# The tails of batches 0 and 1 at the head of SyncE's queue, and a new order of the whole program

## The chip, the core and the metric

One core of one Trainium2 chip runs the whole program in one launch. The metric is the device time of one execution in microseconds. The time before is the median of three runs, 277.85 us (277.29 to 281.95).

## The reference, cut to what matters

```
q, k, v: (8 batches, 8 heads, 576 rows, 64), float32
phi(x) = where(x > 0, x, exp(x) - 1) + 1
kv  = sum over rows of phi(k)^T v          # 64 x 64 per head
z   = sum over rows of phi(k)
att = phi(q) kv / (phi(q) z + 1e-6)
x   = att as (4608, 512)
a = x @ w1;  b = x @ w2                    # 512 -> 1024
out = (a * b) @ w3 @ w_out                 # 1024 -> 1024 -> 512
```

## The kernel before

Each batch's 576 rows are cut into a main part of 512 rows (four row groups of 128) and a **tail** of 64 rows. The main part of q, k or v is one load of 1 MB (step `ld`, line 119) into one of five buffers. A tail is 128 KB, fetched as 64 x 8 pieces of 256 bytes; tails of two batches share the 128 partitions of one of four buffers, so there are four pairs (0,1), (2,3), (4,5), (6,7). Step `lr` (line 127) loads one tail, step `lp` (line 135) both tails of a pair as two DMAs.

phi is computed as min(max(x, 0) + 1, exp(x)): `x` and `xr` are the exponential on ScalarE (main part and tail), `t` and `tr` the max-and-add on VectorE, `m` and `mr` the minimum on VectorE. `v` and `vr` copy v beside a column of ones, so that `kv` (TensorE) sums kv and z in one product: four matmuls over the main part and one over the tail, for each pair of heads. `kc` and `kh` copy the sums out of PSUM. So `kv` of a batch needs the tail of that batch too.

q is transposed by TensorE for batches 0 to 2 (`qt`, `qc`), by a DMA transpose on SyncE's queue for 3 to 7 (`qd`); `na` multiplies by kv, `nd` (VectorE) divides, and the result is transposed again, by TensorE (`xp`, copied by `xc`) for batches 0 to 2, by DMA (`xd`) for the others. Tails of q go the same way in pairs (`qdr`, `nar`, `ndr`, `xdr`).

w3 @ w_out is made once at the start (`l3`, `lo`, `w3t`, `w3c`, `wa`, `wf`, `wc`), so that the feed-forward part has two products. Chunks 0 to 7 are the batches' main parts, chunk 8 all tails. `f:c,i` (line 393) is one of eight column blocks of chunk c: four matmuls for a and four for b; `ac` (ScalarE) copies a out of PSUM, `ab` (VectorE) multiplies by b. `o:c,m` (line 418) is eight matmuls into 128 output rows; `oc` copies and `st` stores them. The first block of chunk 0 is cut into pieces (`fk`), each started when its part of the transposed input is there. The PSUM pool that f, o, qt, xp and w3t share has four buffers.

All steps stand in one string, ORDER (line 451); each engine and each DMA queue executes its instructions in the order of that string, and only data, buffers and semaphores make it wait. GATES (line 522) adds waits by hand: in `A<B` the load A is issued only when step B is done. SyncE's queue (`,s`) takes most loads, all stores and all DMA transposes; GpSimd's queue (`,g`) takes the weights and the loads of batches 0 and 1, with at most eight DMAs under way.

Of the kernel before, what the change touches and what calls it, by code (L numbers as in the profile page):

```python
# [18 lines left out]
def kernel(  # L19
# [437 lines left out]
    w3c:5,a l3:7 t:k,0,0,4 wf:4 wc:2,v wc:1,a wc:3,a lw:0,0,256 t:k,0,4,4 x:k,0,0,4 wf:5 wc:4,v
    x:k,0,4,4 lw:1,0,256 m:k,0,0,0 m:k,0,0,1 x:q,0,0,4 m:k,0,4,2 t:q,0,0,4 wc:5,a lw:0,1,256 m:q,0,0,1
    x:q,0,4,4 m:q,0,0,0 m:k,0,4,3 qt:0,0,2 t:q,0,4,4 wc:0,a lw:1,1,256 m:q,0,4,2 qc:0,0,2,v lw:0,1,512
    v:0,4,2,a v:0,0,4,v kv:0,2 lw:1,1,512 v:0,6,2,a m:q,0,4,3 kh:0,2,1,a kv:0,1 kh:0,2,0,v kv:0,0 kv:0,3  # L460
    ld:k,1,0,8,g kc:0,0,1,0,a kc:0,0,1,1,v w3t:6 kh:0,3,1,a kh:0,3,0,v na:0,1 na:0,0 w3c:6,a qt:0,2,2
# [100 lines left out]
```

## Time and profile before

| | |
|---|---|
| runs, median (lowest to highest) | 277.85 us (277.29 to 281.95) |
| profiled execution, its own time | 276.11 us |
| its span in the trace | 274.3 us |
| mean granted TensorE clock | 0.960 of 2.4 GHz |
| TensorE / VectorE / ScalarE busy | 243.8 / 164.1 / 125.4 us |
| TensorE in its last stretch, 161 to 270 us | 108.5 us busy of 109 |

The trace is of one execution. Its span reaches from the first to the last instruction; the execution's own time holds 1.8 us more than that. The median of the three runs is 1.7 us above the profiled execution's time. A busy TensorE is a modelled figure, since matmuls are pipelined; a row's idle time (in brackets) names what ended it. A granted clock of 1.00 is 2.4 GHz, one of 0.50 is 1.2 GHz; a value between them is a mean over a stretch that holds both.

### The profile page before, as it was taken

How to read it: one execution, taken by the hardware profiler on the slowest of the kernel's cores; microseconds unless marked ns; L12 is line 12 of the kernel's file. 1: busy time of each engine (PE TensorE's matmuls, PEld its weight loads, DVE VectorE, ACT ScalarE, POOL GpSimd, SP SyncE). 2: the span in 40 equal slices, each digit the busy share in tenths (PEclk: the TensorE clock that was granted, in tenths of full speed). 3: DMA queues.
4: the chain of work that ended last, by engine and by line, in shares of the span. 5: the costliest groups of instructions: out<-in, count | busy, mean ns of one | idle time of the engine just before them, and what ended most of it. 6: DMA issues, size and time to landing. Idle time of an engine off the chain costs nothing.

```text
span 274.3 us, 3971 instructions
## 1 busy us (share of the span) xinstructions
PE 243.8 (89%) x1456; PEld 126.2 (46%) x1474; DVE 164.1 (60%) x366; ACT 125.4 (46%) x190; POOL 21.1 (8%) x35
## 2 busy tenths in 40 slices
PE   6795890998999998779999599999999999999994
PEld 6552740445544553344444244564544444444551
DVE  7308551388998695679899829855975343440110
ACT  3438331478787574364327257823223323333231
POOL 8555500010000000000000000000000000000000
PEclk9999597799999999799999989999999999999998
DMA  6999999896999948999994994891281121003245
GB/s 114 201 291 319 197 260 305 113 352 198 295 273 350 349 145 199 248 220 189 347 265 140 206 307 103 166 182 38 43 163 44 41 59 38 0 2 115 76 133 135
DMA packets 69074, 49.53 MB, mean 181 GB/s; under 512 B 39232, under 2 KB 62016, under 8 KB 69056
## 3 DMA queue, kind: packets, MB, share of 16 engines
q1 hardware_dynamic: 61792, 37.63, 54.2%
q0 software_dynamic: 7120, 11.54, 18.7%
q8 instruction: 11, 0.18, 0.3%
q10 hardware_dynamic: 144, 0.13, 0.1%
q14 instruction: 7, 0.06, 0.1%
HBM read 38.80 MB, written 9.44 MB: 176 GB/s over the span
## 4 chain that ended last, share of the span: by engine, by line
PE 57%; DMA 18%; DVE 15%; issue 4%; ACT 4%; SPq 1%; POOL 1%; DVEq 0%; POOLq 0%; ACTq 0%
PE a_ps L393 19%; PE b_ps L393 17%; PE o_ps L418 14%; DMA k32r<-in_k_dram 4%; DMA k<-in_k_dram 4%; DMA xt<-xn 3%; DVE ab L412 3%; DMA q<-in_q_dram 3%; DVE t L172 3%; DVE xn L299 2%; DMA w3b<-in_moe_w_dram 2%; PE kvp L238 2%; ACT e L166 2%; DVE q L180 2%; DMA q32r<-in_q_dram 2%
## 5 line engine op out<-in xcount | busy, mean ns | idle before, releaser
L393 PEld LDWEIGHTS <-w_sb 128*128 128x128 bf16 x576 | 56.4, 100 | 77.6 <-issue 17.8
L412 DVE TENSOR_TENSOR ab<-a_sb,b_ps 128x512 bf16<-128x512 f32 x72 | 49.1, 684 | 50.5 <-PE b_ps L393 45.8
L393 PE MATMUL a_ps<-xt,w_sb 128*128 128x512 bf16 x256 | 69.0, 391 | 10.7 <-ACT xt L338 7.3
L407 ACT COPY a_sb<-a_ps 128x512 f32<-128x512 f32 x72 | 41.9, 584 | 63.3 <-PE a_ps L393 62.1
L393 PE MATMUL b_ps<-xt,w_sb 128*128 128x512 bf16 x256 | 68.0, 387 | 0.0
L418 PE MATMUL o_ps<-wf_sb,ab 128*128 128x512 bf16 x265 | 63.6, 379 | 2.9 <-DVE ab L412 2.3
L418 PEld LDWEIGHTS <-ab 128*128 128x128 bf16 x280 | 26.3, 98 | 31.8 <-DVE ab L412 3.9
L424 ACT COPY o_sb<-o_ps 128x512 f32<-128x512 f32 x25 | 14.5, 585 | 24.5 <-PE o_ps L418 22.6
L299 DVE TENSOR_TENSOR xn<-nd,r 128x512 bf16<-128x512 f32 x32 | 22.1, 691 | 1.1
L166 ACT ACTIVATE e<-q 128x1024 bf16<-128x1024 f32 x16 | 16.8, 1057 | 9.0 <-DMA q<-in_q_dram 4.9
L166 ACT ACTIVATE e<-k 128x1024 bf16<-128x1024 f32 x16 | 16.5, 1055 | 3.8 <-DVE q L180 2.0
L172 DVE TENSOR_SCALAR t<-k 128x1024 bf16<-128x1024 f32 x16 | 10.8, 685 | 8.1 <-DMA k<-in_k_dram 8.1
L180 DVE TENSOR_TENSOR q<-t,e 128x512 bf16<-128x512 bf16 x32 | 12.7, 419 | 3.9 <-DMA qt<-q 3.1
L291 PE MATMUL nd<-kvb,qt 128*128 128x130 bf16 x128 | 12.2, 226 | 2.3 <-DMA qt<-q 2.2
L238 PE MATMUL kvp<-vt,k 128*128 128x130 bf16 x128 | 11.9, 231 | 2.5 <-ACT vt L217 1.0
L291 PEld LDWEIGHTS <-qt 128*128 128x128 bf16 x128 | 9.3, 100 | 8.3 <-DMA qt<-q 2.6
L180 DVE TENSOR_TENSOR k<-t,e 128x512 bf16<-128x512 bf16 x32 | 12.5, 420 | 0.9 <-ACT e L166 0.7
L238 PEld LDWEIGHTS <-k 128*128 128x128 bf16 x128 | 9.3, 102 | 5.5 <-issue 1.7
L172 DVE TENSOR_SCALAR t<-q 128x1024 bf16<-128x1024 f32 x16 | 10.8, 687 | 1.5 <-DMA q<-in_q_dram 1.4
L424 DVE COPY o_sb<-o_ps 128x512 f32<-128x512 f32 x10 | 6.9, 688 | 7.8 <-PE o_ps L418 7.8
L217 ACT CAST vt<-v 128x1024 bf16<-128x1024 f32 (+1 forms) x11 | 10.1, 932 | 1.9 <-PE kvp L238 1.7
L298 DVE RECIPROCAL r<-r 128x8 f32<-128x8 f32 (+1 forms) x40 | 8.1, 202 | 1.4
(68 smaller groups left out, 187.5 us busy)
## 6 DMA issues: line engine op xcount, KB each, us to landing
out_dram<-o_sb SPq DMA_DIRECT2D x31, 256.0 KB, 3.0
k<-in_k_dram SPq DMA_DIRECT2D x6, 1024.0 KB, 7.0
q<-in_q_dram SPq DMA_DIRECT2D x6, 1024.0 KB, 8.0
v<-in_v_dram SPq DMA_DIRECT2D x6, 1024.0 KB, 8.0
w3b<-in_moe_w_dram POOLq DMA_DIRECT2D x8, 256.0 KB, 8.3
v<-in_v_dram POOLq DMA_DIRECT2D x3, 512.0 KB, 11.0
out_dram<-o_sb SPq DMA_DIRECT2D x9, 128.0 KB, 2.4
k32r<-in_k_dram SPq DMA_DIRECT2D x8, 128.0 KB, 4.9
```

The costliest lines, as they stand in the source:

```text
L166: return nc.scalar.activation(out=e[:, 0:nh * W], in_=raw[n, b][:, h0 * W:(h0 + nh) * W], func=AF.Exp)
L172: nc.vector.tensor_scalar(out=d[:, 0:nh * W], in0=raw[n, b][:, h0 * W:(h0 + nh) * W], scalar1=0.0, scalar2=1.0, op0=ALU.max, op1=ALU.add)
L180: nc.vector.tensor_tensor(out=d[:, hp].rearrange("p j u d -> p u j d"), in0=ts[n, b, h0][:, s].rearrange("p (u j d) -> p u j d", u=2, j=NJ ...
L217: copy_of[eng](out=vts[b % len(vts)][:, :, h0:h0 + nh, 0:D], in_=raw["v", b].rearrange("p (h j d) -> p j h d", h=H, j=NJ)[:, :, h0:h0 + nh])
L238: nc.tensor.matmul(dst, kj[:, hp, j].rearrange("p u d -> p (u d)"), vt[:, j, 2 * hp:2 * hp + 2, :].rearrange("p h e -> p (h e)"), start=(j ...
L291: nc.tensor.matmul(o[:, j // 2, (j % 2) * 256:(j % 2) * 256 + PW], sb["qt", b][:, hp, j * P:(j + 1) * P], kvb[b][:, hp].rearrange("p u e - ...
L299: nc.vector.tensor_tensor(out=dst, in0=o[:, :, :, 0:D], in1=r.unsqueeze(3).to_broadcast(list(r.shape) + [D]), op=ALU.mult)
L393: nc.tensor.matmul(o, w[:, kc, f * P:(f + 1) * P], xt_of(c)[:, :, kc, :], start=(kc == 0), stop=(kc == KC - 1))
L407: return copy_of[eng](out=d, in_=ps["a", c, f])
L412: nc.vector.tensor_mul(out=d[:, f, :], in0=sb["a", c, f], in1=ps["b", c, f])
L418: nc.tensor.matmul(d, sb["ab", c][:, f, m * P:(m + 1) * P], wf_sb[:, f, :], start=(f == 0), stop=(f == FC - 1))
L424: return copy_of[eng](out=d, in_=ps["o", c, m])
```

## The change

The multiset of steps stays the same: the same loads, matmuls, copies and stores, with the same tiles and sizes. Three things differ.

First, the four tail loads of batches 0 and 1 stand at the head of SyncE's queue. Before, the two of batch 1 were held by gates until the last w3 transpose was copied out (`w3c:7`).

Second, all seven old gates are gone (six on tails, one on the second half of v of batch 1); one is new: the main part of q of batch 2 waits until that of q of batch 1 has landed.

Third, the order of all steps is another, and 52 copies change between ScalarE (`a`) and VectorE (`v`), about as many one way as the other.

```
...
-    const:4 lr:k,0,s l3:0 zr:0,1 lr:v,0,s const:0 const:10 const:1 warm:26,0 const:6 l3:1 const:8 l3:2
...
+    const:8 lr:k,0,s l3:0 const:6 lr:v,0,s l3:1 zr:0,0 lr:k,1,s const:0 const:9 l3:2 warm:26,0 lr:v,1,s
...
-    GATES = "lr:k,1,s<w3c:7,a lp:k,1,s<w3c:7,a lr:v,1,s<w3c:7,a lp:v,1,s<ac:0,2,a ld:v,1,4,4,g<ac:0,5,a lp:q,0,s<ac:2,6,a lp:q,1,s<ac:4,3,a"
+    GATES = "ld:q,2,0,8,s<ld:q,1,0,8,g"
```

How the order moves instructions is shown at three places. In a row, `k32r` and `v32r` are tails of k and v, `k_660` and the like main parts, `er` the exponential of a tail, `xt` the transposed input of a chunk.

SyncE's queue at the start of the program, before the change:

```order
L127 DMA k32r<-in_k_dram 64x8x64
L127 DMA v32r<-in_v_dram 64x8x64
L127 DMA k32r<-in_k_dram 64x8x64
L135 DMA k32r<-in_k_dram 64x8x64 x2
L127 DMA v32r<-in_v_dram 64x8x64
L135 DMA v32r<-in_v_dram 64x8x64 x2
L119 DMA k_660<-in_k_dram 128x8x256
```

and with it:

```order
L127 DMA k32r<-in_k_dram 64x8x64
L127 DMA v32r<-in_v_dram 64x8x64
L127 DMA k32r<-in_k_dram 64x8x64
L127 DMA v32r<-in_v_dram 64x8x64
L119 DMA q_672<-in_q_dram 128x8x256
L135 DMA k32r<-in_k_dram 64x8x64 x2
L135 DMA v32r<-in_v_dram 64x8x64 x2
L119 DMA v_785<-in_v_dram 128x8x256
```

The third and fourth tails now stand right behind the first two, with nothing to wait for; the pair (2,3) stands behind the first main part (q of batch 2).

ScalarE around the copies of chunk 0's transposed input, before (kvb is kv of batch 0, a_sb the first a of the feed-forward part):

```order
L365 COPY w3t<-w3p 128x1024 x2
L386 CAST wf_sb<-wf_ps 128x512
L338 COPY xt<-xtp 128x4x128 x2
L194 ACTIVATE er<-k32r 64x512
L338 COPY xt<-xtp 128x4x128
L407 COPY a_sb<-a_ps 128x512 x3
```

With the change, at the start of its program (w3A is the first transposed blocks of w3, vrz the tails of v):

```order
L194 ACTIVATE er<-k32r 64x512
L365 COPY w3A<-w3p 128x1024 x3
L225 CAST vrz<-v32r 64x8x64
L194 ACTIVATE er<-k32r 64x512
L225 CAST vrz<-v32r 64x8x64
```

and around those copies:

```order
L259 CAST kvb_113<-kvp 64x65 x3
L365 COPY w3t<-w3p 128x1024
L338 COPY xt<-xtp 128x4x128
L386 CAST wf_sb<-wf_ps 128x512 x2
L407 COPY a_sb<-a_ps 128x512 x4
```

The exponential of batch 1's tail has gone from between the copies of chunk 0 to the start of the program; three of the four xt copies are VectorE's now.

SyncE's queue in the middle of the program, at the load of v of batch 6 (v_1361 before, v_1746 with the change). Before:

```order
L135 DMA q32r<-in_q_dram 64x8x64 x2
L135 DMA k32r<-in_k_dram 64x8x64 x2
L135 DMA v32r<-in_v_dram 64x8x64 x2
L119 DMA v_1361<-in_v_dram 128x8x256
L135 DMA v32r<-in_v_dram 64x8x64 x2
L279 DMA_TRANSPOSE qt<-q 128x16x128
L343 DMA_TRANSPOSE xt<-xn 128x16x128
```

With the change:

```order
L343 DMA_TRANSPOSE xt<-xn 128x16x128
L279 DMA_TRANSPOSE qt<-q 128x16x128
L436 DMA out_dram<-o_sb 128x512 x2
L135 DMA q32r<-in_q_dram 64x8x64 x4
L119 DMA v_1746<-in_v_dram 128x8x256
L135 DMA q32r<-in_q_dram 64x8x64 x2
L119 DMA k_1794<-in_k_dram 128x8x256
L119 DMA v_1826<-in_v_dram 128x8x256
```

The load of v of batch 6 now stands behind two DMA transposes, two stores and four tails of q.

## Rows read from the trace of the kernel before

**Rows 1.** The page, parts 1 and 2: busy time, and TensorE's in 40 slices.

```profile
PE 243.8 (89%) x1456; PEld 126.2 (46%) x1474; DVE 164.1 (60%) x366; ACT 125.4 (46%) x190; POOL 21.1 (8%) x35
...
PE   6795890998999998779999599999999999999994
```

**Rows 2.** Chain of waits, 30 to 52 us: start, us, what.

```profile
35.26 11.50 DMA k32r<-in_k_dram
...
46.79 0.63 ACT er L194
...
47.44 0.59 ACT xt L338
```

**Rows 3.** TensorE's instructions in time, 40 to 54 us: start, us, group, idle before.

```profile
40.60 0.38 PE L393 MATMUL b_ps<-xt,w_sb 128*128 128x512 bf16 x1
48.08 0.58 PE L393 MATMUL a_ps<-xt,w_sb 128*128 128x512 bf16 x1 [7.10 <-ACT xt L338]
...
51.67 1.03 PE L393 MATMUL a_ps<-xt,w_sb 128*128 128x512 bf16 x4
52.53 1.03 PE L393 MATMUL b_ps<-xt,w_sb 128*128 128x512 bf16 x4
```

**Rows 4.** SyncE's own waits: who for whom, us, times, longest.

```profile
SPq L127 <- ACT w3t L365: 33.1, 1, 33.1
```

**Rows 5.** Table of stretches: us, busy by engine, granted clock, DMA share, GB/s.

```profile
0.00:4.00 4.00, 2.00 (x19) 2.00 (x20) 2.85 (x7) 1.28 (x1) 2.90 (x10) 1.00 0.43 86
4.00:8.00 4.00, 2.72 (x25) 2.28 (x23) 3.51 (x10) 2.08 (x3) 3.44 (x6) 1.00 1.07 167
20.00:24.00 4.00, 3.40 (x16) 1.37 (x14) 3.50 (x7) 3.38 (x6) 2.05 (x3) 1.00 1.03 349
48.08:51.67 3.59, 3.59 (x10) 1.29 (x10) 0.75 (x2) 1.17 (x2) 0.00 (x0) 0.59 1.01 106
111.65:115.92 4.27, 4.27 (x15) 1.60 (x13) 3.43 (x11) 1.75 (x3) 0.00 (x0) 0.60 0.96 219
157.44:160.53 3.09, 3.09 (x8) 1.08 (x8) 0.00 (x0) 1.14 (x2) 0.00 (x0) 0.55 1.08 354
```

**Rows 6.** TensorE's instructions in time, later stretches.

```profile
64.87 0.39 PE L238 MATMUL kvp<-vt,k 128*128 128x130 bf16 x4
...
65.15 0.39 PE L238 MATMUL kvp<-vt,k 128*128 128x130 bf16 x4
...
76.72 1.04 PE L393 MATMUL a_ps<-xt,w_sb 128*128 128x512 bf16 x4
...
111.18 0.63 PE L291 MATMUL nd<-kvb,qt 128*128 128x130 bf16 x8 [2.16 <-DMA qt<-q]
...
123.68 4.71 PE L418 MATMUL o_ps<-wf_sb,ab 128*128 128x512 bf16 x21 [1.61 <-DVE ab L412]
...
157.44 1.86 PE L393 MATMUL a_ps<-xt,w_sb 128*128 128x512 bf16 x4 [3.25 <-DMA xt<-xn]
```

**Rows 7.** ScalarE's instructions in time, 108 to 125 us.

```profile
115.70 0.63 ACT L194 ACTIVATE er<-q32r 128x512 bf16<-128x512 f32 x1 [2.15 <-DMA q32r<-in_q_dram]
```

**Rows 8.** GpSimd's queue in time, the main part of q of batch 1.

```profile
30.32 0.89 POOL L119 DMA_DIRECT2D q<-in_q_dram  x1 [0.36 <-issue]
```

**Rows 9.** The q tiles: DMA transposes (ns shortest/median/longest), and landing times of q loads.

```profile
L279 SPq DMA_TRANSPOSE qt<-q x5: 1993/5462/6934, 103.6 to 174.1; - x5
...
DMA to landing us min/median/max: 5.8/8.0/16.9
```

**Rows 10.** SyncE's queue in time: start, us of issuing, transfer, count.

```profile
52.23 0.48 SPq L119 DMA_DIRECT2D k<-in_k_dram  x1
...
161.93 7.04 SPq L135 DMA_DIRECT2D q32r<-in_q_dram  x6
```

**Rows 11.** The k tiles: landing times of k loads.

```profile
DMA to landing us min/median/max: 5.7/8.0/14.8
```

**Rows 12.** The v tiles: landing times of v loads.

```profile
DMA to landing us min/median/max: 5.6/10.0/18.8
```

More of the change, by code (lines that the diff above doesn't have):

```diff
@@ L457 @@
[L457 to L461, printed above, removed]
@@ new lines @@
+    const:3 l3:3 xr:k,0,0 lo:0,2 const:1 const:4 const:11 lo:2,2 w3t:0 zr:0,1 const:5 warm:8,1 lo:4,2
+    w3c:0,a tr:k,0,0 mr:k,0,0 lo:6,2 const:7 const:2 l3:4 const:10 l3:5 w3t:1 warm:8,2 w3c:1,a
+    ld:k,0,0,4,g w3t:2 warm:8,3 w3c:2,a ld:k,0,4,4,g w3t:3 vr:0,a warm:8,4 w3c:3,v ld:q,0,0,4,g wa:0,1
+    wa:1,1 ld:q,0,4,4,g wa:2,1 xr:k,0,1 tr:k,0,1 mr:k,0,1 wa:3,1 ld:v,0,0,4,g wa:4,1 wa:5,1 ld:v,0,4,2,g
+    vr:1,a wa:6,1 ld:v,0,6,2,g w3t:4 wa:7,1 w3c:4,a l3:6 w3t:5 wc:0,v wc:2,a wf:4 w3c:5,a wc:1,v l3:7
@@ new lines @@
+    xp:0,0 w3t:7 nd:0,2 xc:0,0,a wf:6 ld:v,1,0,4,g w3c:7,v xp:0,1 ld:v,1,4,4,g wf:7 wc:6,a xc:0,1,v
+    na:0,3 xp:0,2 wc:7,a fk:0,0,0,2 nd:0,3 xc:0,2,v xp:0,3 fk:0,0,2,1 xc:0,3,v fk:0,0,3,1 ac:0,0,a f:0,1
+    ab:0,0 ac:0,1,a f:0,3 ab:0,1 ac:0,3,a f:0,5 ab:0,3 ac:0,5,a f:0,7 ab:0,5 x:k,1,0,4 t:k,1,4,4
+    t:k,1,0,4 ac:0,7,a f:0,2 m:k,1,0,1 x:k,1,4,4 m:k,1,0,0 ab:0,7 ac:0,2,a m:k,1,4,2 f:0,6 x:q,1,0,4
+    ld:q,2,0,8,s m:k,1,4,3 ab:0,2 lp:k,1,s x:q,1,4,4 t:q,1,0,4 f:0,4 m:q,1,0,1 ac:0,6,a v:1,0,4,v ab:0,6
@@ new lines @@
+    xp:1,3 st:0,0,s v:2,4,4,a xp:1,2 vr:3,v o:0,1 xc:1,3,v xc:1,2,a m:q,2,0,1 mr:k,1,2 oc:0,3,a
+    ld:v,3,0,8,s v:2,0,4,v vr:2,a f:1,3 m:q,2,0,0 oc:0,1,v ac:1,3,a st:0,3,s t:k,2,4,4 x:k,2,4,4
+    st:0,1,s f:1,0 t:k,2,0,4 x:k,2,0,4 ab:1,3 ld:q,3,0,8,s m:k,2,4,2 ac:1,0,a qt:2,0,2 m:k,2,0,1 f:1,1
+    m:k,2,4,3 qc:2,0,2,a m:k,2,0,0 t:k,3,4,4 x:k,3,0,4 t:k,3,0,4 kv:2,1 ab:1,0 kv:2,3 ac:1,1,a
+    ld:q,4,0,8,s kv:2,0 x:k,3,4,4 kv:2,2 ab:1,1 f:1,6 m:k,3,0,0 kc:2,0,2,1,a m:k,3,4,2 v:3,0,4,a
+    kc:2,0,2,0,v m:k,3,0,1 na:2,3 m:k,3,4,3 na:2,1 ac:1,6,a f:1,4 nd:2,3 v:3,4,4,a ld:v,4,0,8,s nd:2,1
@@ new lines @@
+    ac:1,4,a ab:1,6 xp:2,3 na:2,0 kv:3,1 xc:2,3,a ab:1,4 f:1,7 nd:2,0 x:q,3,0,4 lp:k,2,s t:q,3,0,4
+    ac:1,7,a xp:2,0 m:q,3,0,0 f:1,2 x:q,3,4,4 ab:1,7 xc:2,0,v ac:1,2,a m:q,3,0,1 t:q,3,4,4 x:q,4,4,4
+    xp:2,1 lp:v,2,s na:2,2 ab:1,2 f:1,5 xc:2,1,a m:q,3,4,3 x:q,4,0,4 nd:2,2 ac:1,5,a t:q,4,0,4 kv:3,0
+    xp:2,2 kv:3,2 m:q,3,4,2 xc:2,2,a kv:3,3 ab:1,5 qd:3 o:1,3 kc:3,0,2,1,a t:q,4,4,4 kc:3,0,2,0,a
+    v:4,4,4,a v:4,0,4,v f:2,4 oc:1,3,a st:1,3,s ac:2,4,a f:2,0 xr:k,2,2 tr:k,2,2 ab:2,4 mr:k,2,2
@@ new lines @@
+    na:4,3 oc:1,2,a na:4,0 f:2,7 nd:4,3 st:1,2,s nd:4,0 ac:2,7,a ld:q,5,0,8,s na:4,1 na:4,2 ab:2,7 o:2,2
+    nd:4,1 x:k,5,4,4 t:k,5,4,4 ld:v,5,0,8,s f:3,5 t:k,5,0,4 x:k,5,0,4 oc:2,2,v xr:q,0,2 tr:q,0,2
+    st:2,2,s m:k,5,4,2 ac:3,5,a f:3,4 mr:q,0,2 m:k,5,0,1 ab:3,5 ld:q,6,0,8,s ac:3,4,a m:k,5,4,3 o:2,0
+    m:k,5,0,0 ab:3,4 xr:k,3,2 tr:k,3,2 x:q,5,4,4 t:q,5,4,4 f:3,1 oc:2,0,v x:q,5,0,4 qdr:0 mr:k,3,2
+    m:q,5,4,2 ac:3,1,a nd:4,2 f:3,2 st:2,0,s ab:3,1 v:5,4,4,a xd:4 v:5,0,4,v ac:3,2,a f:3,6 m:q,5,4,3
@@ new lines @@
+    nar:1 ab:4,4 f:4,0 ab:4,6 ac:4,0,a ndr:1 na:5,3 m:q,6,0,0 f:4,7 xdr:0 nd:5,3 ac:4,7,a ab:4,0 qd:6
+    x:k,6,0,4 t:k,6,0,4 f:4,2 tr:q,1,2 xr:q,1,2 m:k,6,0,1 ac:4,2,a ab:4,7 x:k,6,4,4 kv:6,1 t:k,6,4,4
+    f:4,5 ab:4,2 xd:5 m:k,6,4,3 ac:4,5,a m:k,6,4,2 m:k,6,0,0 kv:6,3 kv:6,2 ab:4,5 o:4,2 v:7,4,4,a
+    mr:q,1,2 tr:q,2,2 xr:q,2,2 o:4,0 mr:q,2,2 oc:4,2,a qdr:1 tr:q,3,2 xr:q,3,2 qdr:2 kv:6,0 oc:4,0,v
+    o:4,1 kc:6,0,2,1,a v:7,0,4,a st:4,2,s st:4,0,s kc:6,0,2,0,a o:4,3 oc:4,1,v st:4,1,s na:6,1 oc:4,3,a
@@ new lines @@
+    m:q,7,4,3 qd:7 f:5,0 oc:3,0,a ac:5,0,a st:3,0,s nar:6 nar:7 ab:5,0 f:5,4 ndr:7 ac:5,4,a ndr:6 f:5,7
+    ab:5,4 xdr:3 ac:5,7,a na:6,2 nar:4 ab:5,7 f:5,1 ndr:4 ac:5,1,a nd:6,2 xdr:2 f:5,6 ab:5,1 xd:6
+    ac:5,6,a na:7,1 na:7,3 ab:5,6 o:5,1 nd:7,3 nd:7,1 o:5,3 oc:5,1,a st:5,1,s na:7,0 oc:5,3,v o:5,0
+    nd:7,0 st:5,3,s na:7,2 oc:5,0,v o:5,2 nd:7,2 st:5,0,s xd:7 f:6,6 oc:5,2,v ac:6,6,a st:5,2,s f:6,7
+    ab:6,6 ac:6,7,a f:8,0 ab:6,7 ac:8,0,a f:6,3 ab:8,0 ac:6,3,a f:8,1 ab:6,3 ac:8,1,a f:7,7 ab:8,1
@@ new lines @@
+    ac:7,7,a f:7,6 ab:7,7 ac:7,6,a f:7,4 ab:7,6 ac:7,4,a f:6,2 ab:7,4 ac:6,2,a f:8,3 ab:6,2 ac:8,3,a
+    f:7,5 ab:8,3 ac:7,5,a f:6,4 ab:7,5 ac:6,4,a f:8,2 ab:6,4 ac:8,2,a f:8,6 ab:8,2 ac:8,6,a f:7,2 ab:8,6
+    ac:7,2,a f:7,0 ab:7,2 ac:7,0,a f:7,3 ab:7,0 ac:7,3,a f:6,5 ab:7,3 ac:6,5,a f:7,1 ab:6,5 ac:7,1,a
+    f:8,5 ab:7,1 ac:8,5,a ol:7,3 ab:8,5 o:7,2 o:7,0 oc:7,2,a st:7,2,s o:7,1 oc:7,0,a st:7,0,s f:8,7
+    oc:7,1,v st:7,1,s ac:8,7,a f:6,1 ab:8,7 ac:6,1,a f:8,4 ab:6,1 ac:8,4,a f:6,0 ab:8,4 ac:6,0,a o:8,1
@@ L521 @@
+    ab:6,0 o:6,3 oc:8,1,a st:8,1,s o:8,3 oc:6,3,a st:6,3,s o:8,0 oc:8,3,v st:8,3,s o:8,2 oc:8,0,a
+    st:8,0,s o:6,1 oc:8,2,a st:8,2,s o:6,0 oc:6,1,a st:6,1,s o:6,2 oc:6,0,a st:6,0,s oc:6,2,v st:6,2,s
     """
[L522 removed]
+    GATES = "ld:q,2,0,8,s<ld:q,1,0,8,g"
     ctx.enter_context(tc.manual_schedule())
```

88 lines of the change are left out of this document (25 added, 63 removed).

## The prediction

> **What bounds the kernel now.** The page comes first. TensorE is busy 243.8 of 274.3 us, and its slices stand at 9 nearly everywhere after the first third; the slice that reads 0 is the seventh, near 41 to 48 us [rows 1]. From 161 us on it hardly pauses. So the time is TensorE's own work plus the places at which it stands still, and these are looked for next.
>
> The chain of waits shows the largest place: a 128 KB tail of k takes 11.50 us from its issue at 35.26 to its landing, then 0.63 us of exponential on ScalarE, then a 0.59 us copy of the transposed input [rows 2]. TensorE's own rows show it from the other side: a matmul at 40.60, the next at 48.08, after 7.10 us idle that the copy ended [rows 3]. The copy needs nothing of that tail. It stands behind the tail's exponential on ScalarE, which works in order, and the exponential waits for the DMA. The tail is late because SyncE held it 33.1 us behind the last w3 copy [rows 4].
>
> The table of stretches shows what the pause costs besides. From 48.08 to 51.67 the granted clock is 0.59, a mean of the two levels of 1.2 and 2.4 GHz, and TensorE had stood still for the 7 us before [rows 5]. At full clock the same work takes 0.59 x 3.59 = 2.1 us, so 1.5 us are lost. The whole pause is worth 7.1 + 1.5 = 8.6 us.
>
> Three later pauses have the same form: 2.16 us behind a DMA transpose of q, 1.61 us behind VectorE's product, 3.25 us behind a DMA transpose of x [rows 6]; two are followed by stretches at 0.60 and 0.55, which lose 0.40 x 4.27 = 1.7 and 0.45 x 3.09 = 1.4 us [rows 5]. The second starts on ScalarE, which stands still 2.15 us for a tail of q [rows 7]. Together they cost 10.1 us.
>
> **What the change does, part by part.** No matmul, copy or byte is added or removed, so the sum is about pauses.
>
> *The tails of batch 1.* They no longer wait. ScalarE's exponential of that tail moves to the start of the program, and three of four copies of chunk 0's transposed input go to VectorE. The first feed-forward block then follows its last transpose, copied on VectorE: two more matmuls and a copy after 40.60 come to about 41.3 us. Seven whole blocks stand ready behind it; before, they ran on without a pause once TensorE had restarted.
>
> *The price at the head.* Two more tails, 256 KB in pieces of 256 bytes, go ahead of weights and k. Below: nothing, since the 16 DMA engines are busy only 0.43 in the first 4 us. Above: the rate of the crowded stretch from 4 to 8 us, 167 GB/s, gives 262 KB / 167 = 1.6 us; the best later stretch, 349 GB/s, gives 0.75 [rows 5]. I take 1.2, nearer to the crowded row, because small pieces belong there. The start of chunk 0 is fed by these loads, so all of it is on the path: restart at 41.3 + 1.2 = 42.5. The Trainium skill, "DMA: Bandwidth & Descriptors" (Anatomy of one DMA), prices the moving part at bytes over 436 GB/s, by which this term would be 0.6 us and the sum 0.6 us better; its Specifications say that pieces under 512 B do not reach line rate, which speaks for the upper end and against putting tails first. The trace of before, at 167 GB/s with 256-byte pieces in flight, leans to the second, though casting weight loads run in the same stretch.
>
> *The gain at the first pause.* Before, the restart counts as 48.08 + 1.5 = 49.6 at full clock; with the change, 42.5. That is 7.1 us, between 5.5 (restart at 44.0) and 8.6 (restart at 41.0).
>
> *What is late next.* The main parts of batch 1: GpSimd issues the q at 30.32, and at the longest landing of any q load, 16.9 us, it is there at 47.2 [rows 8, 9]; with 1.2 us for the two tails, 48.4. k is issued ahead of it. Their use stands behind four and six blocks, 7 and 10 us after the restart, so after 49.5. The new gate on q of batch 2 opens with that landing, before 52.23, where SyncE's first main load was issued before [rows 10]. So the loads of batch 2 come no later than now, and I cost them at nothing; if that gate opened 10 us late, ScalarE's exponential of q of batch 2 would stand in the way of stores and copies.
>
> *The three later pauses.* Before the first use of batch 3's q, the order now puts one output step and four blocks, 5 x 1.73 us (a block is two pieces, the first of which takes 52.53 - 51.67 = 0.86 [rows 3]) against 2.0 to 6.9 us of issuing a transpose and a short landing [rows 9]: gone. The tail of q is asked for about ten steps ahead of its exponential: gone. Between the division that feeds chunk 4's transpose and the first block of chunk 4 stand about six steps, 10 us, with another transpose beside it: mostly gone. So 10.1 us can fall away.
>
> *What stands in their place.* SyncE's queue is one line for loads, stores and transposes, and the new order puts main loads behind both. I price the tightest: v of batch 6. VectorE casts it ahead of a product of chunk 4. The last minimum on q of batch 5, which releases the transpose ahead of that load, precedes this cast by seven steps and about seven small groups of four matmuls (0.28 each [rows 6]): 7 x 1.73 + 2.0 = 14.1 us of cover. In that time SyncE must issue the transpose (2.0 to 6.9 us [rows 9]), two stores (1 us), four tails of q (four sixths of 7.04 = 4.7 at most, four times 0.48 = 1.9 at least) and the load, which lands in 5.6 us at the shortest and 10.0 in the median [rows 10, 12]: between 10.5 and 22.6. So it is 3.6 us early to 8.5 us late; I take 2.5 us late, the middle, and 1.4 us of low clock behind it. Two more loads stand like it, k of batch 5 behind a transpose and a store, and k of batch 7 behind four stores; each has about as much cover as its 5.7 to 8.0 us of landing [rows 11], and I take 1.5 us for each, between 0 and 4. That makes 6.9 us, between 2 and 18. The later pauses thus go from 10.1 to 6.9.
>
> *VectorE and ScalarE.* Between chunk 0 and chunk 1 both stay close to full; the copies that change sides are about as many each way and 0.1 us apart. Nothing is taken for them.
>
> **The sum.** 274.3 - 7.1 - 3.2 = 264.0 us of span. The profiled execution took 276.1 with 1.8 us around its span, so 265.8; the median of the runs stands 1.7 us above that. Forecast: **267.5 us**, 3.7% less. Its own range: restart at 41.0 and 2 us of new pauses give 257.7 of span, 261 in the median; restart at 44.0 and 10 us give 268.7, or 272.
>
> **The rivals.** All times are medians (span plus 3.5).
>
> *The first pause goes, the later ones only change place.* Pauses of 10 to 12 us: 274.3 - 7.1 + 1 = 268.2, so 271.7. For it: the order before also left 10.1 us that way. Chance 0.17.
>
> *The gain is given back in the middle.* Pauses of 12 to 19 us, if v of batch 6 and k of batch 5 and 7 come 4 to 5 us late each with 1.4 us of low clock behind: some 17 us, 274.3 - 7.1 + 7 = 274.2, so 277.7. Against it: the longest issues of before fell where loads of 1 MB were under way, and the price above takes their middle already. [...] Chance 0.14.
>
> *Slower.* The mechanism is one: SyncE's line is stopped by a step that needs TensorE's progress, and TensorE needs the load behind it. The place is v of batch 6. It decides from the point where issue and landing together pass the 14.1 us of cover; each us after that is a us of the whole, because the cast sits ahead of VectorE's products. Slower by over 2% (5.6 us) needs 7.1 + 10.1 + 5.6 = 22.8 us of pauses: the 8.5 us at the far end of that sum, and the same at two later loads of the line, 25.5 us or 286.2. Chance 0.05.
>
> *The change doesn't do what it says.* The tails land early but the blocks cannot start, because weights of columns 512 on arrive late (their loads were issued last) or the head is slower than 1.6 us. Then the first pause stays, say 7 of 8.6 us: 274.3 - 1.6 - 3.2 = 269.5, so 273.0. Against it: before, seven blocks ran on the same weights without a wait as soon as TensorE restarted. Chance 0.09.
>
> **How the numbers follow.** The forecast has 0.55. A measurement here can tell about 2%, so the bounds are 272.3 and 283.4. Faster: 0.54 of the forecast, 0.12 of the first rival and 0.03 of the last, 0.69. Within: the rest of these (0.01, 0.05, 0.06) and the second rival, 0.26. Slower: 0.05. The range 261 to 276.5 leaves out the slower case, some 0.05 below and 0.09 of the second rival.
>
> **What would show it.** Right: tails of batch 1 landed before 10 us; no 7 us pause near 41; the first full block at 42 to 44 at a granted clock of 1.00; chunk 1's first block near 67 to 69 instead of 76.7 [rows 6]; the tail of the trace, all matmuls, unchanged in length. Wrong: a new pause between 41 and 55 that ends on a weight or on k or q of batch 1; pauses over 12 us in sum between 100 and 165 that end on a main load through ScalarE or VectorE.

## The result and the profile after

| | before | after |
|---|---|---|
| runs, median (lowest to highest) | 277.57 us (276.03 to 281.95, 4 runs) | 260.49 us (259.28 to 261.56, 4 runs) |
| ratio, 95% interval | | 0.940 [0.934, 0.947] |
| profiled execution / its span | 276.11 / 274.3 us | 260.57 / 258.8 us |
| mean granted clock | 0.960 | 0.986 |

6% faster, where 3.7% was forecast; the median lies 0.5 us under the low end of the range. The page answers [rows 1]: TensorE's busy time fell by 4.0 us and its share rose from 89 to 93%, and the slice that read 0 is gone.

```profile
PE 239.8 (93%) x1474; PEld 125.4 (48%) x1474; DVE 162.2 (63%) x362; ACT 126.3 (49%) x194; POOL 21.7 (8%) x35
...
PE   5589499999999999999999799999999999999993
```

SyncE's queue in time, against [rows 4]: the first line is the tail of batch 1's k, the second that of its v, and nothing holds them. They landed 11.8 and 14.3 us after these issues, at 14.0 and 17.2 us.

```profile
2.22 0.64 SPq L127 DMA_DIRECT2D k32r<-in_k_dram  x1
2.90 0.66 SPq L127 DMA_DIRECT2D v32r<-in_v_dram  x1
```

TensorE's rows at the place of [rows 3] (start, us, group): the last piece of the first block starts at 42.80 and whole blocks run from 43.23. There is no idle time in brackets.

```profile
42.21 0.38 PE L393 MATMUL a_ps<-xt,w_sb 128*128 128x512 bf16 x1
42.43 0.38 PE L393 MATMUL b_ps<-xt,w_sb 128*128 128x512 bf16 x1
42.80 0.38 PE L393 MATMUL a_ps<-xt,w_sb 128*128 128x512 bf16 x1
43.01 0.38 PE L393 MATMUL b_ps<-xt,w_sb 128*128 128x512 bf16 x1
43.23 1.02 PE L393 MATMUL a_ps<-xt,w_sb 128*128 128x512 bf16 x4
```

All later places at which TensorE stood still for 0.3 us or more, and chunk 1's first block (76.72 in [rows 6], now 67.42):

```profile
56.68 0.39 PE L238 MATMUL kvp<-vt,k 128*128 128x130 bf16 x4 [0.35 <-ACT kvb L248]
...
67.42 1.03 PE L393 MATMUL a_ps<-xt,w_sb 128*128 128x512 bf16 x4
...
86.23 0.40 PE L333 MATMUL xtp<-ident,xn 128*128 128x128 bf16 x4 [0.39 <-DVE xn L299]
...
141.95 1.02 PE L393 MATMUL a_ps<-xt,w_sb 128*128 128x512 bf16 x4 [0.41 <-DVE ab L412]
...
147.20 0.40 PE L238 MATMUL kvp<-vt,k 128*128 128x130 bf16 x4 [1.64 <-DVE k L180]
...
167.24 0.40 PE L238 MATMUL kvp<-vt,k 128*128 128x130 bf16 x4 [0.37 <-DVE k L180]
168.71 0.40 PE L291 MATMUL nd<-kvb,qt 128*128 128x130 bf16 x4 [0.45 <-DVE xnr L299]
```

They come to 3.6 us in all. Where [rows 6] has 2.16, 1.61 and 3.25 us, nothing of 0.3 us or more stands now. The table of stretches shows the granted clock behind the first restart, over 100 to 165 us and behind the longest pause left: 1.00 in each, against 0.59, 0.60 and 0.55 in [rows 5].

```profile
43.23:55.31 12.08, 12.08 (x57) 5.49 (x56) 8.49 (x16) 8.45 (x13) 0.00 (x0) 1.00 0.94 283
100.00:165.00 65.00, 62.76 (x377) 31.50 (x375) 49.32 (x115) 32.83 (x50) 0.00 (x0) 1.00 1.02 253
147.20:150.00 2.80, 2.80 (x24) 1.60 (x25) 2.80 (x7) 1.35 (x2) 0.00 (x0) 1.00 1.05 220
```

The loads did come late, as forecast. ScalarE's rows (first k of batch 5, then v and k of batch 6, then k of batch 7) and VectorE's cast of v of batch 6, with the idle time ahead of each:

```profile
111.97 2.01 ACT L166 ACTIVATE e<-k 128x1024 bf16<-128x1024 f32 x2 [1.47 <-DMA k<-in_k_dram]
...
140.60 1.05 ACT L217 CAST vt<-v 128x1024 bf16<-128x1024 f32 x1 [1.50 <-DMA v<-in_v_dram]
...
144.96 1.06 ACT L166 ACTIVATE e<-k 128x1024 bf16<-128x1024 f32 x1 [1.36 <-DMA k<-in_k_dram]
...
165.02 2.00 ACT L166 ACTIVATE e<-k 128x1024 bf16<-128x1024 f32 x2 [1.45 <-DMA k<-in_k_dram]
```

```profile
140.60 0.69 DVE L217 CAST vt<-v 128x1024 bf16<-128x1024 f32 x1 [1.33 <-DMA v<-in_v_dram]
```

Set beside TensorE's rows, these four stops cost it 0, 0.41, at most 1.64 and 0.37 us. That is the point at which forecast and trace part, and the experiments go there.

### The profile page after: what moved, and what is told of

Its sections match the earlier page's. It is cut to its first block, busy times and chain, and to the rows that moved or that the text cites. A ratio compares the mean times of both kernels' runs of the same rounds, so it can differ in the third digit from the quotient of the medians.

```text
span 258.8 us, 3980 instructions
## 1 busy us (share of the span) xinstructions
PE 239.8 (93%) x1474; PEld 125.4 (48%) x1474; DVE 162.2 (63%) x362; ACT 126.3 (49%) x194; POOL 21.7 (8%) x35
## 4 chain that ended last, share of the span: by engine, by line
PE 61%; DVE 15%; DMA 11%; ACT 5%; issue 4%; SPq 2%; POOL 1%; DVEq 0%; ACTq 0%; POOLq 0%
PE o_ps L418 18%; PE a_ps L393 17%; PE b_ps L393 17%; DMA wo<-in_moe_w_out_dram 5%; DVE ab L412 3%; DVE xn L299 3%; DMA q<-in_q_dram 3%; DMA v<-in_v_dram 3%; PE kvp L238 3%; DVE t L172 2%; DVE q L180 2%; ACT e L166 2%; PE nd L291 1%; PE wf_ps L381 1%; DVE r L298 1%
## 5 line engine op out<-in xcount | busy, mean ns | idle before, releaser
L393 PEld LDWEIGHTS <-w_sb 128*128 128x128 bf16 x576 | 55.5, 98 | 63.7 <-issue 1.0
L393 PE MATMUL a_ps<-xt,w_sb 128*128 128x512 bf16 x256 | 66.0, 379 | 0.5 <-DVE ab L412 0.4
L393 PE MATMUL b_ps<-xt,w_sb 128*128 128x512 bf16 x256 | 66.0, 379 | 0.0
L424 ACT COPY o_sb<-o_ps 128x512 f32<-128x512 f32 x23 | 13.4, 584 | 23.7 <-PE o_ps L418 23.7
L424 DVE COPY o_sb<-o_ps 128x512 f32<-128x512 f32 x12 | 8.3, 689 | 21.3 <-PE o_ps L418 16.8
L217 ACT CAST vt<-v 128x1024 bf16<-128x1024 f32 (+1 forms) x12 | 11.1, 946 | 2.9 <-DMA v<-in_v_dram 2.0
```

The source lines that it names most:

```text
L217: copy_of[eng](out=vts[b % len(vts)][:, :, h0:h0 + nh, 0:D], in_=raw["v", b].rearrange("p (h j d) -> p j h d", h=H, j=NJ)[:, :, h0:h0 + nh])
L393: nc.tensor.matmul(o, w[:, kc, f * P:(f + 1) * P], xt_of(c)[:, :, kc, :], start=(kc == 0), stop=(kc == KC - 1))
L424: return copy_of[eng](out=d, in_=ps["o", c, m])
```

## The experiments

Times are medians beside runs of the kernel before on the same chip (276.1 us for experiments 1, 2, 4 and the first timing of 6; 277.4 for 3, 5, 7 and the first timing of 9; 277.3 for 8 and the second timings). A first **whole block** is the first one that is not cut into pieces. In the diffs ORDER is cut to what moves, and the places that a step has left are not always shown.

**1. The tails alone, in the order before.**

```
-    ... zr:0,1 lr:v,0,s const:0 ...
+    ... zr:0,1 lr:v,0,s lr:k,1,s lr:v,1,s const:0 ...
-    GATES = "lr:k,1,s<w3c:7,a lp:k,1,s<w3c:7,a lr:v,1,s<w3c:7,a lp:v,1,s<ac:0,2,a ...
+    GATES = "lp:k,1,s<w3c:7,a lp:v,1,s<ac:0,2,a ...
```

> The order of before, with only the four tails of batches 0 and 1 at the head of SyncE's queue. Theory (ScalarE's line): the first pause of 7.1 us goes, TensorE restarts at 42.5 to 43.5 at full clock, and the later pauses stay: 277.6 - 6.5 = 271 us, between 269 and 273. Rival (the new order as a whole is what pays): under 3 us, 275 or more.

Measured: 270.8 us (270.3 to 272.4), ratio 0.981 [0.975, 0.988]. TensorE's rows: the 7.10 us are gone. The three later pauses stand (2.16, 1.40 and 3.04 us); the longest one between is the second line, 1.10 us where 0.65 stood before.

```profile
43.27 0.38 PE L393 MATMUL a_ps<-xt,w_sb 128*128 128x512 bf16 x1 [0.24 <-ACT xt L338]
...
57.74 1.25 PE L418 MATMUL o_ps<-wf_sb,ab 128*128 128x512 bf16 x5 [1.10 <-DVE ab L412]
```

So early tails are enough to remove the first pause, and that is about a third of the gain.

**2. The exponential moved, the tail still late.** In the order before, `xr`, `tr` and `mr` of batch 1's k go behind the fourth block of chunk 0.

```
-    xr:k,0,1 tr:k,0,1 xp:0,3 fk:0,0,2,1 mr:k,0,1 xc:0,3,a ...
+    xp:0,3 fk:0,0,2,1 xc:0,3,a ...
-    ... f:0,7 ab:0,1 xr:k,1,2 tr:k,1,2 ...
+    ... f:0,7 ab:0,1 xr:k,0,1 tr:k,0,1 mr:k,0,1 xr:k,1,2 tr:k,1,2 ...
```

> The order of before with its late tail; only the exponential, max-and-add and minimum of batch 1's tail of k are moved behind the fourth block of chunk 0, so they no longer stand ahead of the copies. Theory (the line, not the tail's lateness, is what costs): restart at about 41.3, 8 us saved, 269.5 us, between 268 and 272. Rival (the tail has to come early): kv of batch 1 or the exponential's place behind it waits instead, under 3 us saved, 275 or more.

Measured: 274.8 us (271.4 to 275.6), ratio 0.989 [0.978, 1.001]: missed. Whole blocks did start at 42.09, but four blocks later TensorE stood still again. TensorE first, then ScalarE:

```profile
42.09 1.02 PE L393 MATMUL a_ps<-xt,w_sb 128*128 128x512 bf16 x4
...
54.64 1.86 PE L393 MATMUL a_ps<-xt,w_sb 128*128 128x512 bf16 x4 [5.48 <-ACT a_sb L407]
```

```profile
46.80 0.63 ACT L194 ACTIVATE er<-k32r 64x512 bf16<-64x512 f32 x1 [1.33 <-DMA k32r<-in_k_dram]
53.48 0.63 ACT L194 ACTIVATE er<-k32r 128x512 bf16<-128x512 f32 x1 [6.06 <-DMA k32r<-in_k_dram]
```

The moved exponential (64 partitions) waits 1.33 us; the next in ScalarE's line, of the tails of batches 2 and 3 (128 partitions), waits 6.06 us. A stop in an in-order line that is removed uncovers the next late load in that line.

**3. Both late exponentials moved.** The second one goes behind chunk 1's `kh` copies.

```
-    ... ab:0,1 xr:k,1,2 tr:k,1,2 ac:0,7,a ...
+    ... ab:0,1 xr:k,0,1 tr:k,0,1 mr:k,0,1 ac:0,7,a ...
-    ... kh:1,3,0,v kh:1,2,0,v
+    ... kh:1,3,0,v kh:1,2,0,v xr:k,1,2 tr:k,1,2
```

> The order before, with the exponential (and its small followers) of BOTH late tails of k moved on ScalarE: the first (batch 1) to stand behind the fourth block of chunk 0, the second (batch 2) behind chunk 1's kv copies. The tails themselves are still asked for where they were. Theory (a pause is a stop of ScalarE's in-order line at an exponential whose tail has not landed; the earlier run moved one such exponential and the next late tail took its place): restart near 41.5 to 42, no pause of several us near 54, and both stops gone, about 8 us off 276.1: 268 us (266 to 270), pauses near 105 to 155 as before. Rival (the stop is not ScalarE's line but something else that is late by then, weights or the main k and q of batch 1): a pause of 4 us or more still stands between 40 and 60 and less than 3 us is saved: 273 or more.

Measured: 270.6 us (269.9 to 274.4), ratio 0.977 [0.968, 0.986], some 6.5 us less and 0.6 above the expected range. Whole blocks start at 41.14, and the 5.48 us are gone. The profiled execution is the longest of the four, and in it the third late tail, of batch 1's v, stood next (landed 18.0 us after its issue). TensorE, then VectorE:

```profile
58.32 1.89 PE L418 MATMUL o_ps<-wf_sb,ab 128*128 128x512 bf16 x4 [4.29 <-DVE ab L412]
```

```profile
54.74 0.43 DVE L225 CAST vrz<-v32r 64x512 bf16<-64x512 f32 x1 [3.55 <-DMA v32r<-in_v_dram]
```

The rival, weights or main loads, is out: the rows on TensorE's path name a tail each time. Its sign, a pause of over 4 us, did appear, but behind a tail.

**4. One later pause alone.** In the order before, SyncE issues the DMA transpose of chunk 3's q ahead of the load of k of batch 5.

```
-    ld:k,5,0,8,s o:1,3 ... x:k,4,0,4 qd:3 na:2,3 ...
+    o:1,3 ... x:k,4,0,4 qd:3 ld:k,5,0,8,s na:2,3 ...
```

> The order of before with one swap on SyncE's queue: the DMA transpose of q of batch 3 ahead of the load of k of batch 5, instead of behind it. Theory (a transpose stands in SyncE's line behind a load whose buffer is not yet free): the pause at 111 us and its low clock go, 3.9 us saved, 273.7 us. Rival (the transpose is slow because the DMA engines are full): it lands as late as before, within 1 us of 277.6.

Measured: 272.6 us (271.1 to 274.2), ratio 0.987 [0.980, 0.994]. TensorE ran through 107 to 112 us without idle time, and where the clock was 0.60 it is 1.00:

```profile
107.00:112.00 5.00, 5.00 (x31) 2.50 (x29) 3.94 (x11) 3.16 (x5) 0.00 (x0) 1.00 1.07 320
111.65:115.92 4.27, 3.93 (x25) 1.98 (x24) 3.11 (x8) 1.10 (x2) 0.00 (x0) 1.00 1.26 192
```

Pause and low clock leave together: 3.5 us for one swap. The rival is out too: the DMA engines' share is 1.26 in the second line, against 0.96 over the same stretch before [rows 5], and the pause is gone all the same.

**5. Four moves in the order before.** Experiments 3 and 4 in one, the tail of q (`lp:q,0`) without its gate right behind `lp:k,2`, and `ld:q,7` behind chunk 4's transpose (`xd:4`).

```
-    lp:k,2,s xc:1,0,v ...
+    lp:k,2,s lp:q,0,s xc:1,0,v ...
-    ... ab:3,5 ld:q,7,0,8,s f:3,7 ... xd:4 kv:5,0 ...
+    ... ab:3,5 f:3,7 ... xd:4 ld:q,7,0,8,s kv:5,0 ...
```

> The order before with only the local moves that the experiments so far single out: both late exponentials moved as in the kernel above; the division that feeds chunk 3 and its transpose issued ahead of the load of k of batch 5; the tail of q of batch 0's successors asked for without its gate, right behind the third tail of k; the load of q of batch 7 put behind chunk 4's transpose. All else stands as before. Theory (the whole gain is four local stops of in-order lines): 276.1 - 8.3 (first pause with its low clock) - 3.6 (at 111) - 1.6 (at 122) - 4.6 (at 155) = 258, within 256 to 262, thus about the time of the changed kernel. Rival (the newly searched order as a whole pays, the single moves only shift pauses to the next late load): 266 or more, with pauses of 1 to 5 us left at other loads.

Measured: 263.0 us (261.6 to 263.9), ratio 0.951 [0.941, 0.960]; the changed kernel's is 0.940 [0.934, 0.947]. That is 1 us above the expected range and 3 below the rival's. So local stops make most of the gain, 0.049 of 0.060 (of 0.054 in the second timing of the changed kernel, under experiment 6). That the rest of the new order adds the remainder is likely; the intervals overlap, and no run takes it apart. One of the four moves missed. The tail of q landed in time, but a pause of 1.63 us stood where 1.61 had been, behind a tail of v on ScalarE. TensorE, then ScalarE:

```profile
114.25 4.71 PE L418 MATMUL o_ps<-wf_sb,ab 128*128 128x512 bf16 x21 [1.63 <-DVE ab L412]
```

```profile
109.50 0.62 ACT L225 CAST vrz<-v32r 64x512 bf16<-64x512 f32 x1 [2.28 <-DMA v32r<-in_v_dram]
```

VectorE then waited 0.95 us for ScalarE's copy and ran without a break up to the product that ended the pause, so at most 0.95 of the 1.63 us is this stop's. In the trace of before the same tail of v was late already, behind the tail of q of [rows 7]:

```profile
118.93 0.62 ACT L225 CAST vrz<-v32r 64x512 bf16<-64x512 f32 x1 [2.12 <-DMA v32r<-in_v_dram]
```

**6. The changed kernel without its early tails.** Batch 1's tails wait for the last w3 copy again; their exponential and cast go behind chunk 0's blocks.

```
-    ... zr:0,0 lr:k,1,s const:0 const:9 l3:2 warm:26,0 lr:v,1,s
+    ... zr:0,0 const:0 const:9 l3:2 warm:26,0
-    ... wa:2,1 xr:k,0,1 tr:k,0,1 mr:k,0,1 wa:3,1 ... vr:1,a wa:6,1 ...
+    ... wa:2,1 wa:3,1 ... wa:6,1 ...
+    ... w3c:7,v lr:k,1,s lr:v,1,s xp:0,1 ...
+    ... ab:0,7 ac:0,2,a xr:k,0,1 tr:k,0,1 mr:k,0,1 m:k,1,4,2 ... ac:0,4,a vr:1,a ...
+    GATES = "lr:k,1,s<w3c:7,v lr:v,1,s<w3c:7,v ...
```

> The changed kernel, with the tails of batch 1 held behind the last w3 copy again, as before, and their exponential, minimum and copy placed behind the blocks of chunk 0. Theory (line): the early tails pay nothing by themselves and cost about 2 us at the head, so 0 to 2 us less than the changed kernel's 260.5: 258.5 to 260.5. Rival (early tails are what pays): 3 to 7 us more, 263.5 to 267.5.

Measured: 259.3 us (256.6 to 260.6), ratio 0.936 [0.927, 0.944]. No pause of several us came back. Timed once more, beside the changed kernel on one chip:

> The changed kernel itself once more, so that the next two stand against it on the same chip: 260.5 us (259.5 to 261.5) by all theories.

> The changed kernel with batch 1's tails waiting for the last w3 copy again and their exponential behind chunk 0's blocks, timed again in more rounds. Theory (early tails pay nothing by themselves and cost the head 1.4 us, the time by which the first transposes of q stand earlier in the trace without them): 259.1 us (258 to 260), 1 to 1.5 us under the changed kernel. Rival (the early tails are what the gain rests on): 264 or more; rival (they cost the head nothing): no difference to the changed kernel.

Measured: the changed kernel 259.8 us (258.9 to 262.4), ratio 0.946 [0.939, 0.952]; without early tails 260.4 us (259.3 to 261.6), ratio 0.945 [0.941, 0.950]. So the two are the same within what this tells, and my 1 to 1.5 us were not there. The two traces of each show a trade: without early tails the first whole block starts at 39.83 and 41.05 us instead of 43.23 and 41.02, but from there to TensorE's end it takes 213.74 and 213.57 us instead of 211.47 and 212.56. That the gain rests on the early tails is refuted: with the exponential out of the way it is there without them.

**7. k of batch 5 later still.** In the changed kernel, its load goes behind a store and a pair of tails of k.

```
-    kv:4,0 ld:k,5,0,8,s oc:1,0,a ... st:1,0,s ... kc:4,0,2,0,a lp:k,3,s
+    kv:4,0 oc:1,0,a ... st:1,0,s ... kc:4,0,2,0,a lp:k,3,s ld:k,5,0,8,s
```

> The changed kernel with the load of k of batch 5 put one transfer later on SyncE's line, behind a tail of k: about 3 us later. It already came 1.5 us after ScalarE was ready for it, and TensorE did not pause. The prediction's price (each us after the cover is a us of the whole, and a low clock behind it): 3 + 1.4 us more, 264 to 265. Theory now (TensorE has finished blocks and products in its buffers ahead of it, so the first 1 to 2 us of a stop on ScalarE or VectorE cost nothing, and only what goes beyond is lost): a pause of 1 to 2.5 us at that place, 261 to 263.

Measured: 260.7 us (258.9 to 263.9), ratio 0.940 [0.930, 0.949]. That is 0.8 us above the second timing of the changed kernel, with intervals that overlap, and under what either theory gave. The medians alone would say that nothing was lost; the trace, of the longest of the four executions (263.86 us), says more. ScalarE now stood still for 3.79 us instead of 1.47:

```profile
114.83 2.00 ACT L166 ACTIVATE e<-k 128x1024 bf16<-128x1024 f32 x2 [3.79 <-DMA k<-in_k_dram]
```

TensorE's rows there, first of the changed kernel, then of this one:

```profile
111.23 1.89 PE L418 MATMUL o_ps<-wf_sb,ab 128*128 128x512 bf16 x8
...
123.32 0.39 PE L238 MATMUL kvp<-vt,k 128*128 128x130 bf16 x4
```

```profile
111.78 1.89 PE L418 MATMUL o_ps<-wf_sb,ab 128*128 128x512 bf16 x8
...
116.78 1.02 PE L393 MATMUL b_ps<-xt,w_sb 128*128 128x512 bf16 x4 [0.51 <-DVE o_sb L424]
...
122.78 1.02 PE L393 MATMUL b_ps<-xt,w_sb 128*128 128x512 bf16 x4 [0.43 <-ACT a_sb L407]
...
125.64 0.39 PE L238 MATMUL kvp<-vt,k 128*128 128x130 bf16 x4
```

TensorE had an output step (1.7 us) and blocks left to run when ScalarE stopped, so there is no pause of several us. But in small steps the same matmuls take 13.86 us instead of 12.09: 1.8 us lost for 2.3 us more of stop. So there was some 2.0 us of work in hand here, by this one trace, and what goes beyond it counts; that is the middle of the theory's pause of 1 to 2.5 us. The median shows 0.8 us of it, with an interval of some 2.5 us either way.

**8. v of batch 6 later still.** In the changed kernel, its load goes behind that of k of batch 6, and so behind the last pair of tails of q as well.

```
-    ld:v,6,0,8,s f:4,3 ... lp:q,3,s ... nd:5,1
-    ld:k,6,0,8,s ab:4,3 ...
+    f:4,3 ... lp:q,3,s ... nd:5,1
+    ld:k,6,0,8,s ld:v,6,0,8,s ab:4,3 ...
```

> The changed kernel with the load of v of batch 6 put behind the load of k of batch 6 on SyncE's line: v about 3 us later, k some 0.6 us earlier. Before this edit v landed 1.3 us after VectorE was ready for it and TensorE lost 0.4 us. Prediction's price and theory now agree here, because VectorE's products stand behind that cast and TensorE's two buffers are full after about a block: of 3 us, nearly all are lost at that place, a pause of 3 to 3.8 us near 142 instead of 0.4; the pause near 147 (k of batch 6, 1.6 us) shrinks to 0 to 1.6 because k has waited less. Together 262 to 264 us. What differs: the prediction adds a low clock of 1.4 us behind it (264 to 265); the theory from the traces of the changed kernel, where no pause of 1.6 us or less was followed by one, leaves this open. Rival (TensorE has 3 us of work ahead there too, as at k of batch 5): no change, 260 to 261.

Measured: 262.9 us (262.0 to 263.9), ratio 0.954 [0.950, 0.958], 3.0 us more than the changed kernel on the same chip, as expected. VectorE, then TensorE, then the stretches behind it:

```profile
143.56 0.70 DVE L217 CAST vt<-v 128x1024 bf16<-128x1024 f32 x1 [5.48 <-DMA v<-in_v_dram]
```

```profile
144.91 1.86 PE L393 MATMUL a_ps<-xt,w_sb 128*128 128x512 bf16 x4 [4.56 <-DVE ab L412]
```

```profile
144.91:148.00 3.09, 3.09 (x8) 1.13 (x8) 2.86 (x8) 1.78 (x3) 0.00 (x0) 0.50 0.06 15
148.00:152.00 4.00, 4.00 (x20) 1.75 (x18) 4.00 (x9) 2.41 (x4) 0.00 (x0) 0.79 0.93 173
```

VectorE's stop grew by 4.15 us (1.33 to 5.48) and TensorE's pause by 4.15 (0.41 to 4.56). Here the forecast's price holds to the hundredth, past the first 0.9 us, and the low clock comes with it: 0.50 x 3.09 + 0.21 x 4.00 = 2.4 us. All traces that have a late load at this place say the same. VectorE's stop and TensorE's pause are 1.33 and 0.41 or 2.11 and 1.20 us in the changed kernel's two, 1.92 and 1.00 or 2.01 and 1.10 in those of experiment 6, 2.68 and 1.77 in experiment 7, 5.48 and 4.56 here: 0.91 or 0.92 apart each time. The pause at 147 (1.64) is gone in return. The sum, 4.9, is above the 3.0 of the medians. Against the second trace of the changed kernel, where the pause was 1.20 already, it is 3.36 + 2.4 - 1.63 = 4.1, and the part from the first whole block on is 4.1 us longer (216.68 against 212.56); the profiled execution is the longest of its six, 1.0 above their median.

**9. Loads ahead of tails.** The kernel of experiment 6, and v and k of batch 6 ahead of three of the four pairs of tails of q.

```
-    ... st:2,3,s kv:5,1 st:2,1,s ab:3,0 ...
+    ... st:2,3,s kv:5,1 st:2,1,s ld:v,6,0,8,s ld:k,6,0,8,s ab:3,0 ...
```

> The changed kernel with two edits: batch 1's tails wait for the last w3 copy again and their exponential stands behind chunk 0's blocks (as the run before did), and the loads of v and k of batch 6 stand on SyncE's line ahead of three of the four tails of q, instead of behind them. Theory (the pauses near 141 and 147, 0.4 to 1.0 and 1.6 to 1.9 us, are these two loads waiting in line): both go, 2 to 2.9 us less than the 259.3 of the run with the first edit alone: 257 us (255.5 to 258). Rival (DMA bandwidth, not the place in the line, makes them late; or the tails of q come late in their stead): the pauses stay or move by some us, 259 to 261.

Measured: 259.5 us (257.8 to 261.5), ratio 0.938 [0.929, 0.947]: missed. From the first whole block to TensorE's end its trace is 1.8 us shorter than that of experiment 6 (211.95 against 213.74), but the first block came 2.7 us later. Timed again:

> The same, and v and k of batch 6 loaded ahead of three tails of q, timed again in more rounds. In its first trace the part from the first full block on was 1.8 us shorter than without this edit, and the part ahead of it 2.7 us longer at a granted clock of 0.50 between 28 and 36 us, although the order there is the same. Theory (the load's place in the line is worth 1.8 us; the head's clock differs by execution, not by kernel): 257.3 us (256.5 to 258.5), 1 to 2 us under the kernel above. Rival (the low clock belongs to this version): no difference, 259 to 260.

Measured: 258.6 us (255.0 to 259.6), ratio 0.933 [0.926, 0.941], 1.8 us under the kernel without this edit and 1.2 under the changed kernel beside it: the lowest median, 0.1 above the expected range. From the first whole block on its second trace is again shorter than that of experiment 6 (211.65 against 213.57 us), but not than the changed kernel's (211.47 and 212.56). So by these traces the edit pays beside experiment 6; that it beats the changed kernel is not shown, and the intervals overlap. The pause at 142 is gone and 1.0 of the 1.64 us behind it stays, on VectorE's minimum, with no load waited for; only 0.6 of it was the load's.

Not tried: what puts a given execution's head at the low clock (last section).

## Why the prediction was right in kind and wrong in size

| term, us of span | forecast | measured |
|---|---|---|
| first pause with its low clock | -7.1 | -6.8 (49.6 to 42.80) |
| three later pauses with theirs | -10.1 | -10.1 |
| small pauses of before, 0.27 to 0.65 each, six | not counted | -1.65 (2.84 to 1.19) |
| new pauses, what stands in their place | +6.9 | +2.4 (0.41 + 1.64 + 0.37) |
| sum | -10.3 | -16.1; the spans differ by 15.5 |

0.6 us of the other sign are not placed. The measured column is of one trace; a second one of the same kernel has 40.59 for the restart and 2.8 us (1.20 + 1.63) of new pauses.

The forecast is too high by 7.0 us: 4.5 of them are the new pauses, 1.8 the way from span to median (below), 1.65 the small pauses; the first pause and what is not placed go 0.9 the other way. The span of 258.8 us still lies inside the range that the forecast worked out for it, 257.7 to 268.7; the term from span to median carried the measured time below 261.

*First pause: right in mechanism, its size partly luck.* Restart forecast at 42.5, at 42.80 in the trace; experiments 1 and 2 show that ScalarE's line held it. In the second trace the restart is at 40.59, below the low end of 41.0; the granted clock from 32 to 36 us is 0.50 in the first trace and 1.00 in the second. The tails landed at 14.0 and 17.2 us and not before 10, but the chain of waits there runs through the load of w_out (11.91 us), not through them.

*Price at the head: about right, with a wide margin.* The first transposes of q start at 28.45, 28.34, 27.59 and 27.12 us in four traces with early tails, and at 26.92, 27.03, 26.56 and 25.94 in four without: 27.9 against 26.6 in the mean, 1.3 us, beside 1.2 taken. The spread within each four is as large, and it didn't show in the times. In these kernels the tails' exponential and cast also move, and ScalarE waits for them at the head (1.97 and 2.59 us in the first trace). Experiment 1 moves the loads alone: 28.23 in its one trace against 25.77 to 27.14 in five others of the order before, 2.0 us from their mean. By the price of the Trainium skill's "DMA: Bandwidth & Descriptors" (Anatomy of one DMA), bytes over 436 GB/s, which the page gives for GpSimd's path while SyncE issued these tails, the estimate was 0.6 us. These traces lean to the other statement of this page of the Trainium skill (Specifications), that pieces under 512 B fall short of line rate; no run here changes the size of the pieces.

*Later pauses: right, one of them for the wrong stop.* All three left; experiment 4 shows one of them to go for one swap with its low clock. For the second the forecast named the wrong stop: behind the tail of q ScalarE waited for a tail of v, and with the tail of q in time the pause stayed (experiment 5).

*What stands in their place: the step that failed.* The forecast took 6.9 us, between 2 and 18, by the rule "each us after that is a us of the whole", with 1.4 us of low clock; 2.4 us were measured. The lateness was about what was taken for k (1.47 and 1.45 us beside 1.5 each) and less for v (1.33, in the second trace 2.11, beside 2.5; the transpose ahead of it was issued in 1.96 us, the low end of [rows 9]). The price was wrong: lateness on ScalarE or VectorE is not yet lateness of TensorE. At k of batch 5 TensorE lost nothing for a stop of 1.47 us, because an output step and blocks whose inputs were ready ran on; for one of 3.79 it lost 1.8 (experiment 7). At v of batch 6 there was 0.9 us of such work, and from there each us counted (experiment 8). The clock behind the longest pause left was 1.00, so the 1.4 us fell away. k of batch 6, not priced, cost 0.6 (experiment 9).

*From span to median.* The forecast added 3.5 us (1.8 around the span, 1.7 from the profiled execution to the median). The changed kernel's profiled execution lies at its median, so 1.8 of the 7.0 us are this term. The profiled execution of before was a low one of its runs.

*The rivals.* Pauses that only change place: experiments 2, 3 and 5 show that mechanism in the old order, one tail after another, but the new order left it 2.4 us. Given back in the middle and slower: their mechanism is real (experiment 8), at a seventh of the size (2.4 of some 17 us).

## What to carry to other kernels

A late load is priced at the engine that bounds, not at the one that waits: count first what the bounding engine can still run without the waiting engine's output, and charge only what goes beyond it. When one stop in an in-order line is removed, look for the next late item in the same line before booking the gain. Small pauses are to be summed too, and a single profiled execution is no measure of where the median lies. A loss that medians cannot tell can be read from the same stretch of two traces, from one row to the same row in the other, though only for these two executions.

## What the runs showed of the hardware

*One order, two clocks.* The head of experiment 9's kernel, in its two traces (stretch 28 to 36 us; the granted clock is 0.50 in the first line and 1.00 in the second):

```profile
28.00:36.00 8.00, 6.91 (x62) 6.41 (x62) 4.92 (x14) 3.49 (x9) 4.79 (x7) 0.50 1.37 200
```

```profile
28.00:36.00 8.00, 6.42 (x64) 4.31 (x64) 4.43 (x13) 3.08 (x8) 3.48 (x5) 1.00 1.38 200
```

TensorE had stood still for 3.35 and 3.16 us just before. The spans are 258.6 and 254.4 us. Of the 4.2 us between them 3.9 lie ahead of the first whole block (42.58 and 38.65) and 1.1 of these ahead of the first transposes of q, so up to 2.8 go with the low clock: much of the spread of about 4 us between executions of these kernels may sit here, and it hid differences of 1 to 2 us.

*Pauses and the clock.* Behind the pause of 1.64 us at 147 the clock was 1.00; behind those of 4.56 (experiment 8) and 5.48 us (experiment 2) TensorE's matmuls took 1.9 us for four instead of 1.03.

*Issuing behind large loads.* The same six tails of q took SyncE 4.43 us to issue ahead of two 1 MB loads (experiment 8) and 9.69 us behind them (in both traces of experiment 9; the line is of the second):

```profile
128.69 4.43 SPq L135 DMA_DIRECT2D q32r<-in_q_dram  x6
```

```profile
127.28 9.69 SPq L135 DMA_DIRECT2D q32r<-in_q_dram  x6
```
